# Attention of the first two batches in a new order, normalisation behind the gates, and stores on another queue

## The chip, the cores and the metric

The kernel runs on one core of a Trainium2 chip. The metric is the time of one execution on the device in microseconds (us). Below, PE is TensorE (matrix products), DVE is VectorE, ACT is ScalarE, POOL is GpSimd and SP is SyncE, which here only issues DMAs.

## The reference

Eight batches, eight heads, 576 positions (seq), head dimension 64, model width 512. Attention has no softmax, so that k and v of a head are first multiplied with each other:

```python
kv = np.einsum('bhsd,bhse->bhde', k, v)
out = np.einsum('bhsd,bhde->bhse', q, kv)
x = out / np.sqrt(np.mean(out * out, axis=-1, keepdims=True) + 1e-6) * g_norm   # (8, 576, 512)
# gated part: a causal convolution of 5 taps along seq, for each channel
gate = 1 / (1 + np.exp(-sum(conv_w[k] * xp[:, k:k + S] for k in range(5))))
x = gate * (x @ w_val) @ w_out
# second part
theta = x @ w_theta
y = w_tok_r @ (x * cos(theta)) + w_tok_i @ (x * sin(theta))
u = x + y
out = u + np.maximum(u @ w_ch, 0)
```

q, k, v arrive as float32, the weights as float64.

## The kernel before

Everything is held transposed, with channels on partitions: x of a batch is a tile of 128 partitions by 4 channel blocks by 576 positions. A weight is loaded in four chunks; each chunk comes as 64-bit words and is decoded to float32 on DVE by integer operations (`decode`, L94 to L96 and L98, with one ACT pass at L97), and then split in a high and a low part (`parts`, L68 on ACT and L69 on DVE; the names end in h and l). Every large product is made of three matmuls, high by high, high by low and low by high (`product`, L274 to L276).

The span has two parts. The first makes x, the gate and the w_out result of each batch, and stores the latter to DRAM (yd). The second loads these back and does theta, the mixing of positions and w_ch; the change does not touch it. In the first part the loop over batches i runs, for each i:

- four v products (`value`, L274 to L276 with `wv`; 24 matmuls for each of four channel blocks m). Behind each, DVE multiplies the product by the gate (L288), and ACT and DVE split it (gh, gl). The gate of a block is one ACT copy (L263), four taps on DVE (L265) and a sigmoid on ACT (L266).
- between them, attention of batch i+2: kvp (`key_value`, L182, 80 small matmuls, copied to kvs by ACT at L185) ahead of v1; o (L200, 4 groups of 8 matmuls) in two steps, the second behind the last v; ACT squares each o (L204) and copies it, scaled by g_norm (gsb), into x (L205).
- x of batch i+1 is normalised (`normalize`). For batches 0 and 1 the inverse root is spread over the partitions by matmuls (yb, L254), for the others through DRAM: a store rd (L228) and two broadcast loads yb (L233). DVE multiplies (L257 or L246), and ACT and DVE split the result in xh and xl, which the next v products read.
- four w_out products y (`first`, with `wo`). y0 and y1 first take three of their four input blocks and then the fourth. ACT copies y to yo (L304), and SP stores it (L305). After y1, `between` makes the sums of squares of batch i+2 (ss, L212) and the chain of eleven small DVE operations that makes the inverse root (L219 to L225).
- a chunk of w_theta and up to three pieces of w_tok are decoded with a low priority, the latter to be stored to DRAM (td).

Ahead of the loop stand the loads (the order is the string START: k blocks carry k and v of a pair of heads, q blocks q, v and o chunks of `wv` and `wo`, c the taps), key_value(0), three of `wv`'s four chunks, the taps, attention(0), normalize(0), then key_value(1) and attention(1). Loads of k and v use four buffers, of q two. The four PSUM tiles of this part (pool pd) are handed out in turn. A scheduler keeps the order of priorities of the code, and places an operation where its engine is free by its estimates; `issue_after` holds operations behind a named instruction. All DMAs of this part but a few are issued by SP.

## Time and profile before

| | |
|---|---|
| median of 3 runs | 753.28 us (752.94 to 756.45) |
| the profiled execution's own time | 753.31 us |
| its span | 751.5 us, 1.8 less than its time |
| PE busy | 709.7 us, 94% |
| DVE busy | 523.9 us, 70% |
| ACT busy | 335.9 us, 45% |
| start of the first v product | 48.53 us |
| start of the second part | 315.2 us |

The page gives busy times over the span. A row of the windows answer has the stretch, its length, busy time (and instructions) of PE, PE's weight loads, DVE, ACT and POOL, PE's granted clock as a share of full speed, the share of the DMA engines that was busy, and GB/s. A row of waits has who waited for whom, the total us, how often, and the longest. A timeline row has the start, the duration, the engine, the line and the operation, and in brackets how long the engine had been idle and what released it. A row of the chain of waits has start, duration and what it was. A row of groups has the line, the operation with its shape, its count, then the busy time in us and the mean ns of one. A row of DMA issues ends with the size of one and the median us from issue to landing.

### The profile page before, as it was taken

The page shows a single profiled execution, that of the slowest core. Times are in us where ns is not written, and L with a number is a line of the kernel's source. Part 1 is how long each engine was busy: PE and PEld are TensorE (multiplying, and loading weights), DVE is VectorE, ACT ScalarE, POOL GpSimd, SP SyncE. Part 2 cuts the span into 40 slices and gives each one's busy share as a digit, 9 for nine tenths or more (in the row PEclk, how much of TensorE's full clock was granted, in tenths as well). Part 3 has the DMA queues.
Part 4 walks back from the last instruction along what each step waited for, and adds up shares of the span by engine and source line. Part 5 has one row for each costly group of instructions (what it writes and reads, how often), then busy time and mean ns, then how long its engine had stood idle before and what let it go on. Part 6 is the DMA issues. An engine that isn't in the chain of part 4 may idle for free.

```text
span 751.5 us, 14674 instructions
## 1 busy us (share of the span) xinstructions
PE 709.7 (94%) x6000; PEld 669.9 (89%) x6000; DVE 523.9 (70%) x930; ACT 335.9 (45%) x560; POOL 20.7 (3%) x72
## 2 busy tenths in 40 slices
PE   1679999999989999889999999999999999999998
PEld 1568999798987999879899899999999998998998
DVE  6389969798879999588983872853853835836504
ACT  2366565637464645376541640621622514514301
POOL 4000000000000000000000000000000000000000
PEclk9779999999999999999999999999999999999999
DMA  9948794979896358534345034163051270160101
GB/s 256 285 140 243 209 229 141 229 228 237 219 238 189 108 136 246 190 102 122 111 138 157 9 119 113 32 174 90 17 164 59 69 179 35 64 175 1 64 1 64
DMA packets 77059, 104.88 MB, mean 140 GB/s; under 512 B 11712, under 2 KB 42560, under 8 KB 76992
## 3 DMA queue, kind: packets, MB, share of 16 engines
q1 hardware_dynamic: 76416, 101.85, 48.5%
q0 software_dynamic: 576, 2.10, 0.9%
q8 instruction: 47, 0.77, 0.4%
q14 instruction: 20, 0.16, 0.1%
HBM read 72.73 MB, written 31.19 MB: 138 GB/s over the span
## 4 chain that ended last, share of the span: by engine, by line
PE 60%; DVE 24%; DMA 8%; ACT 4%; issue 3%; SPq 1%; POOL 0%; DVEq 0%; ACTq 0%; POOLq 0%
PE u L513 10%; PE u L511 10%; PE u L512 10%; DVE acc L265 10%; PE c L276 5%; PE c L274 5%; PE c L275 5%; DMA yb<-rd 4%; PE th L459 3%; PE th L457 3%; PE th L458 3%; DMA kv<-in_kvm_dram 2%; DVE x L246 2%; DVE xl L69 2%; DVE acc L288 2%
## 5 line engine op out<-in xcount | busy, mean ns | idle before, releaser
L516 DVE TENSOR_TENSOR f<-u,f 128x288 f32<-128x288 f32 x64 | 26.5, 455 | 129.8 <-PE u L513 129.8
L265 DVE SCALAR_TENSOR_TENSOR acc<-x,cw,acc 128x576 f32<-128x576 f32 x128 | 100.8, 817 | 1.3 <-ACT acc L263 1.3
L68 ACT ACTIVATE uh<-f 128x288 fp32r<-128x288 f32 x64 | 26.2, 444 | 152.4 <-DVE f L516 152.3
L274 PE MATMUL y<-gh,woh 128*128 128x288 f32 x256 | 77.8, 304 | 7.8 <-DVE acc L288 5.4
L274 PE MATMUL v<-xh,wvh 128*128 128x288 f32 x256 | 77.6, 303 | 0.7 <-DVE acc L288 0.7
L276 PE MATMUL v<-xl,wvh 128*128 128x288 f32 x256 | 76.5, 299 | 0.0
L276 PE MATMUL y<-gl,woh 128*128 128x288 f32 x256 | 75.8, 298 | 0.5 <-DVE gl L69 0.5
L275 PE MATMUL y<-gh,wol 128*128 128x288 f32 x256 | 76.0, 297 | 0.0
L275 PE MATMUL v<-xh,wvl 128*128 128x288 f32 x256 | 76.0, 297 | 0.0
L274 PE MATMUL c<-uh,wch 128*128 128x288 f32 x256 | 75.4, 295 | 0.0
L276 PE MATMUL c<-ul,wch 128*128 128x288 f32 x256 | 75.4, 295 | 0.0
L275 PE MATMUL c<-uh,wcl 128*128 128x288 f32 x256 | 75.4, 294 | 0.0
L274 PEld LDWEIGHTS y<-gh,woh 128*128 128x128 f32 x256 | 48.8, 191 | 11.9 <-DVE acc L288 6.1
L274 PEld LDWEIGHTS v<-xh,wvh 128*128 128x128 f32 x256 | 48.7, 190 | 4.6 <-issue 1.7
L459 PE MATMUL th<-wth,yl 128*128 128x512 f32 x128 | 50.3, 393 | 0.0
L458 PE MATMUL th<-wtl,yh 128*128 128x512 f32 x128 | 50.1, 391 | 0.0
L457 PE MATMUL th<-wth,yh 128*128 128x512 f32 x128 | 50.0, 391 | 0.0
L276 PEld LDWEIGHTS y<-gl,woh 128*128 128x128 f32 x256 | 48.4, 190 | 1.2 <-DVE gl L69 1.2
L276 PEld LDWEIGHTS v<-xl,wvh 128*128 128x128 f32 x256 | 48.6, 190 | 0.3 <-issue 0.2
L275 PEld LDWEIGHTS y<-gh,wol 128*128 128x128 f32 x256 | 48.8, 191 | 0.0
L275 PEld LDWEIGHTS v<-xh,wvl 128*128 128x128 f32 x256 | 48.7, 190 | 0.0
L275 PEld LDWEIGHTS c<-uh,wcl 128*128 128x128 f32 x256 | 48.0, 188 | 0.3
(188 smaller groups left out, 1946.0 us busy)
## 6 DMA issues: line engine op xcount, KB each, us to landing
kv<-in_kvm_dram SPq DMA_DIRECT2D x32, 512.0 KB, 8.6
q<-in_qt_dram SPq DMA_DIRECT2D x32, 288.0 KB, 8.9
yd<-yo SPq DMA_DIRECT2D x32, 288.0 KB, 2.4
f<-yd SPq DMA_DIRECT2D x32, 288.0 KB, 3.7
out_dram<-f SPq DMA_DIRECT2D x64, 144.0 KB, 1.8
sd<-fT SPq DMA_DIRECT2D x64, 128.0 KB, 2.5
yt<-sd SPq DMA_DIRECT2D x8, 1024.0 KB, 5.6
yb<-rd SPq DMA_DIRECT2D x12, 576.0 KB, 8.0
```

What stands on the lines that cost most here:

```text
L68: one = nc.scalar.activation(h, src, AF.Copy)
L265: nc.vector.scalar_tensor_tensor(a, x[:, m, k:k + S], cw[:, m * 5 + k:m * 5 + k + 1], a, ALU.mult, ALU.add)
L274: nc.tensor.matmul(ps, wh[:, m, ks], xh[:, k, tsl], start=(k == 0), stop=False)
L275: nc.tensor.matmul(ps, wl[:, m, ks], xh[:, k, tsl], start=False, stop=False)
L276: nc.tensor.matmul(ps, wh[:, m, ks], xl[:, k, tsl], start=False, stop=(k == 3))
L457: nc.tensor.matmul(ps, yh[:, k, :], wth[0][:, k, :], start=(k == 0), stop=False)
L458: nc.tensor.matmul(ps, yh[:, k, :], wth[1][:, k, :], start=False, stop=False)
L459: nc.tensor.matmul(ps, yl[:, k, :], wth[0][:, k, :], start=False, stop=(k == 3))
L511: nc.tensor.matmul(ps[:, :HS], zh[:, ms], wkh[:, j, sl], start=(i == 0), stop=False)
L512: nc.tensor.matmul(ps[:, :HS], zh[:, ms], wkl[:, j, sl], start=False, stop=False)
L513: nc.tensor.matmul(ps[:, :HS], zl[:, ms], wkh[:, j, sl], start=False, stop=(i == 8))
L516: nc.vector.tensor_tensor(f[:, m, sl], ps[:, :HS], f[:, m, sl], ALU.add)
```

## The change

- The loads start in another order: q's first pairs come ahead of the third k block, and only chunk 0 of `wv` ahead of k and q. gsb is loaded by ACT's queue.
- key_value(0) copies each half of kvp to kvs as soon as it is done, and attention(0) goes by pairs of heads (g) in the outer loop, so that its first two o groups need only the first half. For batch 0 the scaled copy of o into x is on DVE, the squares stay on ACT.
- Of `wv` only chunk 0 is decoded ahead of attention(0). Chunks 1 to 3 come behind normalize(0), in turn with the taps of batch 0.
- key_value(1) and attention(1), which stood ahead of the first v product, are now between the v products of batch 0: key_value(1) behind the second, the two steps of o around the fourth. Loads of batch 2 follow key_value(1).
- normalize(i+1) is held behind the last split of the gated product (gs[2][-1]), and the chunks of `wo` behind the second one.
- ss and the inverse root of batch i+2 come ahead of the last chunk of y0 and y1.
- The stores of yo and of decoded w_tok are issued by ACT's queue.

The diff, cut to its core (the loop over n in attention replaces those over h and g):

```diff
-START = "v0 k0 k1 v1 k2 k3 v2 q0 q1 q2 q3 c0 v3 o0 k4 k5 k6 k7 o1 q4 q5 q6 q7 o2 o3"
-WVFIRST = 3
+START = "v0 k0 k1 q0 q1 k2 k3 q2 q3 v1 c0 v2 v3 k4 k5 k6 k7 o0 q4 q5 q6 q7 o1 o2 o3"
...
+            if b == 0 or g == 1:
+                gs = slice(2 * g if b == 0 else 0, 2 * g + 2)
+                nc.scalar.activation(kvs_of[b][:, gs, :], ps[:, 0:NP * D].rearrange("p (a e) -> p a e", e=D)[:, gs], AF.Copy)
...
+        for n in range(4):
+            g, h = divmod(n, 2) if b == 0 else (n % 2, n // 2)
...
+            if b == 0:
+                nc.vector.tensor_scalar(xo, o, gsb, None, ALU.mult)
+            else:
+                nc.scalar.activation(xo, o, AF.Copy, scale=gsb)
+            if n % 2:
+                yield x
...
-                nc.sync.dma_start(out=ydram[b][:, m, :], in_=yo)
+                nc.scalar.dma_start(out=ydram[b][:, m, :], in_=yo)
         part(0, range(3))
         part(1, range(3))
+        between()
         part(0, (3,))
         part(1, (3,))
-        between()
...
     key_value(0, kvs.pop(0))
-    for k in range(WVFIRST):
-        weight_chunk(px, wv, w_val, k, "wv", raw=raw[f"v{k}"])
+    weight_chunk(px, wv, w_val, 0, "wv", raw=raw["v0"])
+    *_, xy = attention(0, qs)
+    *_, (xs, last) = normalize(0, *xy)
     nc.vector.tensor_copy(cw, decode(px, raw["c0"], NM * 5, "cw", "c"))
-    *_, xy = attention(0, qs.pop(0))
-    *_, (xs, last) = normalize(0, *xy)
-    key_value(1, kvs.pop(1))
-    *_, xy = attention(1, qs.pop(1))
-    sg = [conv(0, m, xs[0]) for m in range(EARLY)]
-    with tc.issue_after(last.ins):
-        for n in range(WVFIRST, 4):
+    sg = []
+    for n in range(1, NM):
+        with tc.issue_after(last.ins):
             weight_chunk(px, wv, w_val, n, "wv", raw=raw[f"v{n}"])
-    kvs[2], qs[2] = load_kv(2), load_q(2)
+        if n <= EARLY:
+            sg.append(conv(0, n - 1, xs[0]))
...
+        def between(m, done):
+            if i == 0 and m == 2:
+                with tc.issue_after(done.ins):
+                    key_value(1, kvs.pop(1))
...
+        if i == 0:
+            *_, xy = second
+            kvs[2], qs[2] = load_kv(2), load_q(2)
+            key_value(2, kvs.pop(2))
+            kvs[3] = load_kv(3)
+            next(ahead)
...
-            *_, (nxs, last) = normalize(i + 1, *xy)
+            with tc.issue_after(gs[2][-1].ins):
+                *_, (nxs, last) = normalize(i + 1, *xy)
         if i == 0:
-            for k in range(4):
-                weight_chunk(px, wo, w_out, k, "wo", raw=raw[f"o{k}"])
+            with tc.issue_after(gs[2][1].ins):
+                for k in range(4):
+                    weight_chunk(px, wo, w_out, k, "wo", raw=raw[f"o{k}"])
...
-                for _ in range(RATE[0] if i < 6 else 8):
+                for _ in range(RATE[0]):
...
-                        nc.sync.dma_start(out=tokdram[:, sl], in_=decode(px, raw, sl.stop - sl.start, f"tk_{j}"))
+                        nc.scalar.dma_start(out=tokdram[:, sl], in_=decode(px, raw, sl.stop - sl.start, f"tk_{j}"))
```

Three places show what the scheduler makes of it. In the rows, names end in the batch, the block m and a running number. First, DVE in the head, from the normalisation of batch 0 on, before (acc0_0 is the gate of batch 0's block 0 in the making, L265 its taps):

```order
L257 TENSOR_TENSOR x0_282<-yb0_0_0_367,x0_282 128x2x288
L257 TENSOR_TENSOR x0_282<-yb0_0_1_377,x0_282 128x2x288
L257 TENSOR_TENSOR x0_282<-yb0_1_0_389,x0_282 128x2x288
L69 TENSOR_TENSOR xl0_366<-x0_282,xh0_365 128x4x288
L257 TENSOR_TENSOR x0_282<-yb0_1_1_399,x0_282 128x2x288
L265 SCALAR_TENSOR_TENSOR acc0_0_537<-x0_282,cw_61,acc0_0_537 128x576
L265 SCALAR_TENSOR_TENSOR acc0_1_544<-x0_282,cw_61,acc0_1_544 128x576
L69 TENSOR_TENSOR xl0_366<-x0_282,xh0_365 128x4x288
L265 SCALAR_TENSOR_TENSOR acc0_0_537<-x0_282,cw_61,acc0_0_537 128x576
L265 SCALAR_TENSOR_TENSOR acc0_1_544<-x0_282,cw_61,acc0_1_544 128x576
L265 SCALAR_TENSOR_TENSOR acc0_0_537<-x0_282,cw_61,acc0_0_537 128x576
```

and now (wv_1 is chunk 1 of `wv`; L271 are the taps, L93 to L97 the decode, L68 the splits):

```order
L263 TENSOR_TENSOR x0_260<-yb0_0_1_355,x0_260 128x2x288
L263 TENSOR_TENSOR x0_260<-yb0_1_0_367,x0_260 128x2x288
L68 TENSOR_TENSOR xl0_344<-x0_260,xh0_343 128x4x288
L263 TENSOR_TENSOR x0_260<-yb0_1_1_377,x0_260 128x2x288
L93 TENSOR_SCALAR dst_wv_1_396<-raw_wv_1_170 128x512
L271 SCALAR_TENSOR_TENSOR acc0_0_404<-x0_260,cw_61,acc0_0_404 128x576
L94 SCALAR_TENSOR_TENSOR dst_wv_1_396<-raw_wv_1_170,dst_wv_1_396 128x512
L68 TENSOR_TENSOR xl0_344<-x0_260,xh0_343 128x4x288
L95 SCALAR_TENSOR_TENSOR dst_wv_1_396<-raw_wv_1_170,dst_wv_1_396 128x512
L271 SCALAR_TENSOR_TENSOR acc0_0_404<-x0_260,cw_61,acc0_0_404 128x576
L97 SCALAR_TENSOR_TENSOR dst_wv_1_396<-raw_wv_1_170,dst_wv_1_396 128x512
L271 SCALAR_TENSOR_TENSOR acc0_0_404<-x0_260,cw_61,acc0_0_404 128x576
```

Between the taps of the first gate now stands the decode of `wv`'s chunk 1, which before had been made ahead of the normalisation.

Second, DVE at the end of batch 1's v products, before (L288 are the gates, L246 the normalisation of x of batch 2, dst_wt a chunk of w_theta):

```order
L288 TENSOR_TENSOR acc1_2_1095<-v1_2_1196,acc1_2_1095 128x576
L69 TENSOR_TENSOR gl1_1066<-acc1_2_1095,gh1_1065 128x576
L246 TENSOR_TENSOR x2_740<-x2_740,yb2_992 128x4x288 x2
L94 TENSOR_SCALAR dst_wt_0_1481<-raw_wt_0_1479 128x512
L288 TENSOR_TENSOR acc1_3_1189<-v1_3_1242,acc1_3_1189 128x576
L95 SCALAR_TENSOR_TENSOR dst_wt_0_1481<-raw_wt_0_1479,dst_wt_0_1481 128x512
L69 TENSOR_TENSOR xl2_1293<-x2_740,xh2_1292 128x4x288
L69 TENSOR_TENSOR gl1_1066<-acc1_3_1189,gh1_1065 128x576
L69 TENSOR_TENSOR xl2_1293<-x2_740,xh2_1292 128x4x288
```

and now (L296 are the gates, L252 the normalisation):

```order
L296 TENSOR_TENSOR acc1_2_1096<-v1_2_1197,acc1_2_1096 128x576
L68 TENSOR_TENSOR gl1_1067<-acc1_2_1096,gh1_1066 128x576
L296 TENSOR_TENSOR acc1_3_1190<-v1_3_1243,acc1_3_1190 128x576
L68 TENSOR_TENSOR gl1_1067<-acc1_3_1190,gh1_1066 128x576
L252 TENSOR_TENSOR x2_769<-x2_769,yb2_975 128x4x288 x2
L93 TENSOR_SCALAR dst_wt_0_1482<-raw_wt_0_1480 128x512
L68 TENSOR_TENSOR xl2_1294<-x2_769,xh2_1293 128x4x288 x2
L271 SCALAR_TENSOR_TENSOR acc2_0_1466<-x2_769,cw_61,acc2_0_1466 128x576
```

The normalisation, which reads yb2, has moved from ahead of the last gate to behind the last split.

Third, ACT in batch 1's w_out products, before (L304 copies y to yo, L266 are the sigmoids of batch 2's gates):

```order
L304 ACTIVATE yo1_0_1344<-y1_0_1300 128x576
L304 ACTIVATE yo1_1_1353<-y1_1_1319 128x576
L266 ACTIVATE acc2_0_1465<-acc2_0_1465 128x576
L266 ACTIVATE acc2_1_1472<-acc2_1_1472 128x576
L304 ACTIVATE yo1_2_1434<-y1_2_1409 128x576
L266 ACTIVATE acc2_2_1546<-acc2_2_1546 128x576
L304 ACTIVATE yo1_3_1462<-y1_3_1437 128x576
L266 ACTIVATE acc2_3_1640<-acc2_3_1640 128x576
```

and now (L313 are the stores, L272 the sigmoids):

```order
L312 ACTIVATE yo1_0_1398<-y1_0_1301 128x576
L313 DMA yd1_71<-yo1_0_1398 128x576
L312 ACTIVATE yo1_1_1407<-y1_1_1320 128x576
L313 DMA yd1_71<-yo1_1_1407 128x576
L272 ACTIVATE acc2_0_1466<-acc2_0_1466 128x576
L312 ACTIVATE yo1_2_1435<-y1_2_1410 128x576
L313 DMA yd1_71<-yo1_2_1435 128x576
L272 ACTIVATE acc2_1_1473<-acc2_1_1473 128x576
L312 ACTIVATE yo1_3_1463<-y1_3_1438 128x576
L313 DMA yd1_71<-yo1_3_1463 128x576
L272 ACTIVATE acc2_2_1547<-acc2_2_1547 128x576
```

Each store stands right behind its copy, ahead of the next copy and of the sigmoids.

More of the change, by code (lines that the diff above doesn't have):

```diff
@@ L173, in key_value @@
         ps = one_bank(f"kvp{b}")
+        kvs_of[b] = pa.tile([P, NP, D], F32, tag="kvs", bufs=2, name=f"kvs{b}")
         for g in range(2):
@@ L183, in key_value, with attention @@
                                          start=(c == 0), stop=(c == 4), tile_position=(0, j * D))
-        kvs_of[b] = pa.tile([P, NP, D], F32, tag="kvs", bufs=2, name=f"kvs{b}")
-        nc.scalar.activation(kvs_of[b], ps[:, 0:NP * D].rearrange("p (a e) -> p a e", e=D), AF.Copy)
-    def attention(b, q):
-        kv = kvs_of.pop(b)
+            if b == 0 or g == 1:
+                gs = slice(2 * g if b == 0 else 0, 2 * g + 2)
+                nc.scalar.activation(kvs_of[b][:, gs, :], ps[:, 0:NP * D].rearrange("p (a e) -> p a e", e=D)[:, gs], AF.Copy)
+    def attention(b, qs):
+        kv, q = kvs_of.pop(b), qs.pop(b)
         x = pa.tile([P, NM, PAD + S], F32, tag="x", bufs=2, name=f"x{b}")
@@ L275, in product @@
             nc.tensor.matmul(ps, wl[:, m, ks], xh[:, k, tsl], start=False, stop=False)
-            nc.tensor.matmul(ps, wh[:, m, ks], xl[:, k, tsl], start=False, stop=(k == 3))
+            done = nc.tensor.matmul(ps, wh[:, m, ks], xl[:, k, tsl], start=False, stop=(k == 3))
+        return done
     def value(b, x, xh, xl, sg, between):
@@ L280, in value @@
         gl = pa.tile([P, NM, S], F32R, tag="gl", bufs=1, name=f"gl{b}")
+        lasts, done = [], None
         for m in range(NM):
-            between(m)
+            between(m, done)
             g = sg[m]
@@ L285, in value @@
             for h in range(2):
-                product(ps[:, h], wv, m, xh, xl, h * HS)
+                done = product(ps[:, h], wv, m, xh, xl, h * HS)
             halves = lambda t: t.rearrange("p (h s) -> p h s", h=2)
             nc.vector.tensor_tensor(halves(g), ps, halves(g), ALU.mult)
-            parts(gh[:, m, :], gl[:, m, :], g)
+            lasts.append(parts(gh[:, m, :], gl[:, m, :], g)[0])
             if m + EARLY < NM:
                 sg.append(conv(b, m + EARLY, x))
-        return gh, gl
+        return gh, gl, lasts
     def first(b, gh, gl, between):
@@ L362, in attention_moe_holo_kernel @@
     raw = {}
+    nc.scalar.dma_start(out=gsb[0:D], in_=gn)
+    nc.scalar.dma_start(out=gsb[D:P], in_=gn)
     for what in START.split():
@@ L401, in attention_moe_holo_kernel @@
         if two:
-            ahead = attention(i + 2, qs.pop(i + 2))
-        def between(m):
-            if two and m == 1:
+            ahead = attention(i + 2, qs)
+        def between(m, done):
+            if i == 0 and m == 2:
+                with tc.issue_after(done.ins):
+                    key_value(1, kvs.pop(1))
+            if two and i and m == 1:
                 key_value(i + 2, kvs.pop(i + 2))
@@ L410, in between @@
             if two and m == 3:
-                next(ahead)
+                next(ahead if i else second)
+        second = attention(1, qs) if i == 0 else None
         gs = value(i, *xs, sg, between)
+        if i == 0:
[4 more added lines that the diff above has]
+            next(ahead)
         if two:
@@ L418, in attention_moe_holo_kernel @@
         if i + 1 < B:
-            *_, (nxs, last) = normalize(i + 1, *xy)
+            with tc.issue_after(gs[2][-1].ins):
+                *_, (nxs, last) = normalize(i + 1, *xy)
         if i == 0:
-            for k in range(4):
-                weight_chunk(px, wo, w_out, k, "wo", raw=raw[f"o{k}"])
+            with tc.issue_after(gs[2][1].ins):
+                for k in range(4):
+                    weight_chunk(px, wo, w_out, k, "wo", raw=raw[f"o{k}"])
         got = []
-        first(i, *gs, lambda: got.append(next(ahead) if two else None))
+        first(i, *gs[:2], lambda: got.append(next(ahead) if two else None))
         xy = got[-1]
@@ L434, in attention_moe_holo_kernel @@
                         weight_chunk(px, w, src, k, name, scale)
-                for _ in range(RATE[1] if i < 6 else 11):
+                for _ in range(RATE[1]):
                     if toks:
```

24 lines of the change are left out of this document (9 added, 15 removed).

## Prediction

> **What bounds the kernel now.** I read the page first (which engine is full), then one windows answer cut at the starts of the eight v products, then PE's waits, and last the timeline at the places where PE waits. PE is TensorE, DVE is VectorE, ACT is ScalarE.
>
> ```profile
> span 751.5 us, 14674 instructions
> PE 709.7 (94%) x6000; PEld 669.9 (89%) x6000; DVE 523.9 (70%) x930; ACT 335.9 (45%) x560; POOL 20.7 (3%) x72
> ```
>
> PE is idle for 751.5 − 709.7 = 41.8 us in all: with the same products a new order wins no more, except where PE's clock is low. The windows answer has one row for the head (up to the first v product), one for each batch 0 to 7, and one for the second part:
>
> ```profile
> 0.00:48.50 48.50, 22.51 (x384) 18.68 (x384) 28.52 (x51) 20.37 (x33) 10.90 (x42) 0.88 0.94 258
> 48.50:89.50 41.00, 40.89 (x466) 36.57 (x465) 38.07 (x74) 24.75 (x40) 1.51 (x5) 0.94 0.74 199
> 89.50:121.60 32.10, 32.10 (x370) 30.05 (x369) 25.96 (x45) 18.18 (x28) 1.18 (x5) 1.00 0.73 187
> 121.60:155.80 34.20, 32.68 (x370) 30.09 (x369) 29.58 (x51) 19.48 (x30) 1.19 (x5) 1.00 0.85 219
> 155.80:189.00 33.20, 32.42 (x370) 29.97 (x370) 29.98 (x51) 19.34 (x31) 1.80 (x5) 1.00 0.84 223
> 189.00:224.10 35.10, 32.39 (x370) 30.04 (x369) 27.70 (x48) 18.02 (x28) 1.45 (x5) 1.00 0.89 223
> 224.10:258.90 34.80, 32.79 (x370) 30.05 (x370) 34.45 (x62) 21.41 (x34) 0.39 (x1) 1.00 0.52 159
> 258.90:286.10 27.20, 25.96 (x194) 25.49 (x193) 25.66 (x44) 14.18 (x23) 0.00 (x0) 1.00 0.51 146
> 286.10:315.20 29.10, 27.18 (x194) 26.95 (x193) 22.48 (x33) 10.75 (x17) 1.22 (x2) 0.94 0.68 211
> 315.20:751.50 436.30, 430.75 (x2930) 412.00 (x2928) 261.50 (x484) 169.42 (x301) 1.06 (x2) 1.00 0.31 91
> ```
>
> Of a row I use the length and the busy times of PE, DVE and ACT. Over half of the span is the second part, which the change leaves alone. The head has 26 us of idle PE. Batch 1 takes 32.10 us with PE busy throughout, so 32.10 is what a batch costs without a gap; batches 2 to 5 take 2.1, 1.1, 3.0 and 2.7 more, 8.9 together. Batches 6 and 7 (no attention left to compute) have 1.24 and 1.92 us of idle PE.
>
> PE's waits name the owners:
>
> ```profile
> PE kvp L182 <- DMA kv<-in_kvm_dram: 16.0, 4, 6.6
> PE y L274 <- DVE acc L288: 5.4, 3, 2.5
> PE ss L212 <- ACT sq L204: 4.7, 3, 3.3
> ```
>
> **Part 1, the head.** The chain up to the first v product, from the chain of waits and the timeline:
>
> ```profile
> 2.54 6.00 DMA kv<-in_kvm_dram
> 8.55 10.79 DMA kv<-in_kvm_dram
> 19.38 2.41 PE kvp L182 x38
> 22.25 2.62 PE L200 MATMUL o<-q,kvs 64*64 64x288 f32 x32 [0.47 <-ACT kvs L185]
> 23.43 0.65 ACT L204 ACTIVATE sq<-o 128x576 f32<-128x576 f32 x1 [1.23 <-PE o L200]
> 28.02 0.78 ACT L205 ACTIVATE x<-o,gsb 128x576 f32<-128x576 f32 x1
> 28.22 0.69 PE L212 MATMUL ss<-sq,ind 128*32 128x72 f32 x28 [0.85 <-ACT sq L204]
> 31.97 4.79 PE L254 MATMUL yb<-y,sel 32*128 32x72 f32 x64 [3.06 <-DVE y L225]
> 37.00 1.36 DVE L69 TENSOR_TENSOR xl<-x,xh 128x1152 fp32r<-128x1152 f32 x1 [0.30 <-ACT xh L68]
> ```
>
> ACT makes four squares (0.65) and four scaled copies (0.78) in a row, and the second half of ss waits for the last square. Now the copies go to DVE, and the first pairs' squares are done before the fourth k block lands. That landing ended at 19.34; I put it at 18.3, an estimate, since a weight chunk less shares the queue with it. From there: half of kvp 2.4, a copy of kvs 0.4, the first o 0.6 (a quarter of 2.62), two squares 1.3, the last ss 0.7, which ends at 23.7; with q's second pairs a little later, 24.2. The rsqrt chain (3.06) then ends at 27.25, where it ended at 31.97: 4.7 earlier (3.7 if the landing stays). Normalisation takes as long as it did (31.97 to the end of the first xl at 38.36), so v0_0 can start at about 33.7. It started at 48.53:
>
> ```profile
> 36.69 4.10 PE L182 MATMUL kvp<-kv 128*64 128x64 f32 x80
> 41.30 2.22 PE L200 MATMUL o<-q,kvs 64*64 64x288 f32 x32 [0.51 <-ACT kvs L185]
> 47.43 1.17 PE L212 MATMUL ss<-sq,ind 128*32 128x72 f32 x28 [3.31 <-ACT sq L204]
> 48.53 0.61 PE L274 MATMUL v<-xh,wvh 128*128 128x288 f32 x1
> ```
>
> PE's clock under that kvp is the third number from the right, 0.50:
>
> ```profile
> 36.00:38.00 2.00, 2.00 (x32) 1.87 (x32) 1.70 (x2) 2.00 (x3) 0.00 (x0) 0.50 0.91 202
> ```
>
> So the first v product moves 14.8 us ahead, and with it the wait of 3.31 goes. But kvp1, o1 and ss1 now come behind it: 2.4 (kvp at full clock; 3.3 of its 4.10 here are at half clock), 2.2 and about 0.7, some 5.3 us. If PE alone set the pace, 14.8 − 5.3 = 9.5 would be won. It doesn't, for DVE is full over the same stretch:
>
> ```profile
> 34.00:95.30 61.30, 57.10 (x754) 51.01 (x752) 57.63 (x102) 36.31 (x56) 3.10 (x12) 0.89 0.71 195
> ```
>
> The price of a decode, from the groups by shape (mean ns of one behind the busy time):
>
> ```profile
> L95 DVE SCALAR_TENSOR_TENSOR dst_tk<-raw_tk,dst_tk 128x512 int32<-128x512 int32 x10 | 6.9, 692 | 0.1
> L94 DVE TENSOR_SCALAR dst_tk<-raw_tk 128x512 int32<-128x512 int32 x10 | 4.2, 425 | 0.0
> ```
>
> DVE idles for 61.30 − 57.63 = 3.67 us from its first read of yb to the last tap of batch 1. That work (normalisation, taps, gates, decodes) now starts 4.7 earlier, but two more decodes stand in it. Only wv's chunk 0 is decoded early now; the early ones cost nothing, since DVE had nothing else then. A decode is five passes, one of 0.425 and four of 0.692; neighbours overlap by about 0.08 (each starts before the last one's end), so 0.35 + 4 × 0.61 = 2.8. So 5.6 us come in, and the end of the stretch moves by −4.7 + 5.6 = +0.9 if it keeps its idle time, and by 0.9 − 3.67 = −2.8 if it loses all of it. PE's earlier start lets DVE lose most, as the gates find their products done: I take −1.6. Instead, PE will wait for wvl and for gates between the products of batch 0.
>
> The 0.94 in batch 0's row is a low clock:
>
> ```profile
> 48.00:50.00 2.00, 2.00 (x24) 1.56 (x13) 2.00 (x4) 2.00 (x5) 0.00 (x0) 0.50 0.28 99
> ```
>
> It follows PE's wait of 3.31 and lasts into v0; the first v product after a shorter wait may keep its clock, which DVE's bound hides either way. The Trainium skill (TensorE: Matmul & The Clock Gate, section "Part 1: The HAM clock gate (the "warmup" mystery)") says that the clock is halved after an idle window of about 3.4 us and released after as long of sustained work. This row agrees, after a wait of 3.31; by the rule a cold start of v0 would cost an estimated 1.7 us.
>
> **Part 2, batches 1 to 5.** Batch 4 shows the excess:
>
> ```profile
> 209.07 2.63 DVE L246 TENSOR_TENSOR x<-x,yb 128x1152 f32<-128x1152 f32 x2 [3.40 <-DMA yb<-rd]
> 211.62 0.75 DVE L288 TENSOR_TENSOR acc<-v,acc 128x576 f32<-128x576 f32 x1
> 212.43 0.40 PE L274 MATMUL y<-gh,woh 128*128 128x288 f32 x1 [2.51 <-DVE acc L288]
> ```
>
> The normalisation of the next batch stands ahead of the last gate on DVE: DVE waits 3.40 for the broadcast yb, multiplies for 2.63, and only then gates; y waits 2.51 for that gate. Now the gates come first, and y needs nothing of the normalisation. Next v needs xl: gate, gh and gl 2.2 (three passes of 0.75), then 2.63 and about 3.8 for xh and two xl of 1.36, 8.6 us behind the last v product. Beside it run y's four tiles of 3.24 each (25.96 in batch 6 is eight such tiles), 13.0, and ss: over 4 us are spare, which also cover yb's wait of 3.40. And rd is sent before y0's last chunk, with no kv load between rd and yb on SP's queue. If that cover went, the next v would wait for what is left of yb. DVE's load in batches 1 to 4 is 25.96 to 29.98 of 32.10, so its queue drains in each batch; I leave 0.3 us of loose joints in each of 2, 3 and 4: 2.1 + 1.1 + 3.0 − 0.9 = 5.3 won. Batch 5 has 34.45 of DVE, and by the order keeps about as much: 34.45 − 32.10 = 2.35 stays of its 2.7, 0.35 won. Together 5.65. Bounds: all 8.9, or nothing if each wait moves to v.
>
> **Part 3, batches 6 and 7.**
>
> ```profile
> 274.95 0.75 DVE L288 TENSOR_TENSOR acc<-v,acc 128x576 f32<-128x576 f32 x1
> 302.51 0.40 PE L274 MATMUL y<-gh,woh 128*128 128x288 f32 x1 [1.92 <-DVE acc L288]
> ```
>
> In batch 6 the last gate (274.95) stands in the order behind passes that decode w_tok; in batch 7 the taps are late and PE waits 1.92, after which PE's clock halves (0.94 in that row). The order now has 10 fewer decode passes between the last gates of batches 5 and 6, 10 × 0.61 = 6.1 us less ahead of those taps, more than the wait. Batch 6 wins 1.0 of its 1.24, batch 7 its distance to batch 6's busy time: 29.10 − 25.96 = 3.1, of which I take 2.9. Bounds: 0 and 4.4.
>
> **Part 4, the stores.** 32 stores of yo and the decoded tokens go to ACT's queue. SP loses the issues:
>
> ```profile
> yd<-yo SPq DMA_DIRECT2D x32, 288.0 KB, 2.4
> q<-in_qt_dram SPq DMA_DIRECT2D x32, 288.0 KB, 8.9
> ```
>
> SP isn't on PE's path in those stages, and what waited behind a store there was the next loads, which land in time. ACT must wait for its own copy to end and issue; its load is 18 to 21 us of 32.10, so I count nothing. No row shows a store from ACT. Below, the bound is the 0.3 a batch that I left in part 2, if yb leaves earlier still; above, ACT waits out the landing of each, 4 × 2.4 = 9.6 a batch, which its 11 to 14 free us still cover. I take nothing, as neither end reaches PE. The Trainium skill (DMA: Bandwidth & Descriptors, section "Issuing engines are not separate DMA queues") says that transfers started by different engines share the same 16 DMA engines, and only time on the issuing sequencer is saved. By that the transfers themselves gain nothing; no row of before can show it, and the sum counts nothing for them.
>
> **The sum.** 1.6 + 5.65 + 1.0 + 2.9 = 11.15 us off the profiled execution, whose own time is 753.31 (1.8 beside its span, 0.03 above the median of the runs): 742.2. Bounds of the terms together: a loss of 0.9, or a gain of 2.8 + 8.9 + 4.4 = 16.1: 754.2 and 737.2.
>
> **The rivals.** *PE sets the head alone:* DVE's idle time disappears, and the decodes fit in gaps between taps, so that the head gives 9.5 instead of 1.6: 734.3. Against it is DVE's row (57.63 of 61.30). Chance 0.07. *The work is only moved:* DVE's total is unchanged, so the stalls come back at v, which then waits for xl in place of y for the gate; only the head's 1.6 and 1.2 of batches 6 and 7 remain: 750.5. For it speaks DVE's 34.45 in batch 5, against it the 2 to 6 us a batch that DVE has spare in batches 1 to 4. Chance 0.14. *k and v of batch 2 come late:* their loads now go out only when kvp1, behind v0_1, has freed the buffers, and kvp2 wants them two v tiles, o1 and ss1 later, some 10 us, where a k block took 6.0 to 10.8 to land; with the 6.6 us wait of kvp's row as a worst case, 4.5 lost: 746.7. Chance 0.08.
>
> *Slower: ACT is held at its stores.* In this trace a transfer starts only when the eighth before it has landed: the chain has one issued at 2.54 landing at 8.54, and the k block that comes eight transfers later issued at 8.55. A store that follows a q or kv load by eight would hold ACT until that lands, and copies of y (which free PSUM tiles), squares and sigmoids queue behind it. It decides where the stores of a batch wait more than about 9.6 us together (y2, y3 and the next v0, 3 × 3.2, pass before v1 wants a tile whose copy is held). With one landing of 8.9 and half of a second, 13.4 − 9.6 = 3.8 lost in each of six batches, 22.8: 765. Against it: the stores come late in y, when the loads of their batch have had 10 us to land. Chance 0.05.
>
> **How the numbers follow.** The forecast has 0.66, with its own range of 737 to 747. 0.5% is 3.8 us, about what a measurement of this kernel can tell from no change: faster is below 749.5, slower above 757.1. Faster: 0.65 of the forecast, the first rival's 0.07, the third's 0.07, 0.02 of the second: 0.81. Same: 0.12 of the second, 0.01 and 0.01 of the forecast and the third: 0.14. Slower: 0.05. The range leaves out ACT's rival (0.05), most of the first (0.06) and the upper half of the second: 735 to 751.
>
> **What would show it.** In the profile after: v0_0 near 34, but v1_0 only 1 to 3 us before 89.56; DVE still full from about 29 to 94; no y waiting for a gate in batches 1 to 4 and no wait of DVE for yb ahead of a gate; batches 2 to 4 near 32.4 each; no low clock in batch 7; a second part of 436.3. I am wrong if v1_0 starts before 84 (PE's head), if v waits for xl by over 1 us a batch, or if ACT's idle time names its own DMA issues.

## The result and the profile after

The changed kernel takes 758.44 us (median of 8 runs, 757.11 to 759.91) where the kernel before takes 754.98 (8 runs, 752.16 to 756.51): a ratio of 1.0053, with a 95% interval of 1.0032 to 1.0074. It is slower by half a per cent, where I had forecast 742.2. The profiled execution took 758.88, 5.6 us more than that of before (753.31).

The page of the changed kernel starts so:

```profile
span 757.1 us, 14657 instructions
PE 716.5 (95%) x6000; PEld 673.2 (89%) x6000; DVE 527.1 (70%) x934; ACT 334.8 (44%) x557; POOL 19.2 (3%) x72
```

PE is busy 6.8 us longer with the same 6000 matmuls, so part of the loss is a lower clock. The windows answer, cut at the starts of the v products as before (head, batches 0 to 7, second part; the head now ends at 33.8, so batch 0 holds what had been ahead of it):

```profile
0.00:33.80 33.80, 16.85 (x240) 12.63 (x240) 13.84 (x30) 7.24 (x13) 9.49 (x38) 0.81 0.96 268
33.80:91.30 57.50, 50.86 (x608) 44.07 (x609) 54.90 (x100) 35.65 (x56) 2.35 (x9) 0.88 0.72 207
91.30:123.40 32.10, 32.10 (x370) 30.05 (x369) 24.38 (x40) 17.71 (x27) 1.23 (x5) 1.00 0.68 187
123.40:155.50 32.10, 32.10 (x370) 30.05 (x369) 31.01 (x53) 19.04 (x30) 1.23 (x5) 1.00 0.83 236
155.50:193.80 38.30, 34.74 (x370) 31.45 (x369) 30.54 (x53) 20.66 (x32) 1.24 (x5) 0.91 0.75 221
193.80:234.10 40.30, 35.02 (x370) 31.86 (x369) 31.95 (x56) 20.54 (x32) 1.23 (x5) 0.92 0.68 204
234.10:268.20 34.10, 32.41 (x370) 29.94 (x369) 31.89 (x56) 20.68 (x33) 0.12 (x1) 1.00 0.40 119
268.20:295.20 27.00, 26.05 (x194) 25.58 (x193) 24.77 (x40) 12.98 (x20) 0.00 (x0) 1.00 0.66 198
295.20:322.80 27.60, 25.82 (x195) 25.56 (x194) 22.87 (x34) 11.66 (x18) 1.22 (x2) 1.00 0.70 206
322.80:757.10 434.30, 430.52 (x2930) 411.99 (x2928) 260.96 (x484) 168.64 (x300) 1.05 (x2) 1.00 0.30 89
```

Against the rows of before: head and batch 0 together 91.3 instead of 89.5 (+1.8), batch 1 as it was, batch 2 −2.1, batch 3 +5.1, batch 4 +5.2, batch 5 −0.7, batch 6 −0.2, batch 7 −1.5, the second part −2.0. These make +5.6, all of the difference. The loss is in batches 3 and 4: PE idles there for 3.6 and 5.3 us, and is busy 2.6 and 2.9 us longer than in batch 1, at a mean clock of 0.91 and 0.92. The head has a low clock too (0.88 in the row of batch 0): 4.3 of PE's 6.8 us lie ahead of batch 1 (67.7 us busy there, 63.4 before).

PE's and DVE's waits name who is late. In the kernel before, DVE waited for yb:

```profile
DVE x L246 <- DMA yb<-rd: 6.2, 3, 3.4
```

and now:

```profile
PE o L202 <- DVE acc L296: 7.2, 2, 4.3
PE y L280 <- DVE acc L296: 1.8, 1, 1.8
...
DVE dst_tk L93 <- DMA td<-dst_tk: 6.9, 2, 5.0
DVE dst_wt L93 <- DMA td<-dst_tk: 5.6, 1, 5.6
```

The wait of y for a gate has shrunk as forecast (5.4 before), and in its place o waits for one. And DVE now waits 12.5 us for stores of decoded w_tok (td) to land. The timeline of batch 3 shows the chain (ACTq is ScalarE's DMA queue; the number ahead of the engine is the duration):

```profile
164.79 0.33 ACTq L458 DMA_DIRECT2D td<-dst_tk  x1
172.87 0.43 DVE L93 TENSOR_SCALAR dst_tk<-raw_tk 128x512 int32<-128x512 int32 x1 [5.05 <-DMA td<-dst_tk]
174.48 0.75 DVE L296 TENSOR_TENSOR acc<-v,acc 128x576 f32<-128x576 f32 x1
175.29 1.24 PE L202 MATMUL o<-q,kvs 64*64 64x288 f32 x8 [2.85 <-DVE acc L296]
```

and the windows answer PE's clock behind it:

```profile
176.00:178.00 2.00, 1.29 (x16) 0.30 (x8) 1.23 (x2) 2.00 (x5) 0.00 (x0) 0.50 0.06 9
```

A store goes out at 164.79, in the middle of the loads of k and v, and lands 8.1 us later. The decode of the piece after next (a w_theta chunk takes the other buffer in between) wants the same one of two buffers (dst), so its first pass waits 5.05 us for that landing; the gate of v behind it on DVE comes at 174.48, and o waits 2.85 for the PSUM tile that the gate frees. PE's clock then falls to 0.50. The Trainium skill (TensorE: Matmul & The Clock Gate, section "Part 1: The HAM clock gate (the "warmup" mystery)") says that the clock is halved after a window of about 3.4 us without work; here a wait of 2.85 was enough, so the trace differs. Nor does the length of a single wait decide it: the 1.8 that y waits in batch 7 left the clock alone, while in the kernel before a wait of 1.92 in batch 7 halved it and one of 2.51 in batch 4 did not (0.94 and 1.00 in their rows).

### The profile page after: what moved, and what is told of

Same layout as the page of the kernel before. It is cut to its first block, busy times and chain, and to the rows that moved or that the text cites. A ratio compares the mean times of both kernels' runs of the same rounds, so it can differ in the third digit from the quotient of the medians.

```text
span 757.1 us, 14657 instructions
## 1 busy us (share of the span) xinstructions
PE 716.5 (95%) x6000; PEld 673.2 (89%) x6000; DVE 527.1 (70%) x934; ACT 334.8 (44%) x557; POOL 19.2 (3%) x72
## 4 chain that ended last, share of the span: by engine, by line
PE 60%; DVE 22%; DMA 9%; ACT 5%; issue 2%; SPq 0%; ACTq 0%; DVEq 0%
PE u L531 10%; PE u L529 10%; PE u L530 10%; DVE acc L271 9%; PE c L280 4%; PE c L281 4%; PE c L282 4%; PE th L477 3%; PE th L475 3%; PE th L476 3%; DMA td<-dst_tk 3%; DMA kv<-in_kvm_dram 2%; DVE xl L68 2%; DVE acc L296 2%; DVE gl L68 1%
## 5 line engine op out<-in xcount | busy, mean ns | idle before, releaser
L271 DVE SCALAR_TENSOR_TENSOR acc<-x,cw,acc 128x576 f32<-128x576 f32 x128 | 102.7, 814 | 1.0 <-ACT acc L269 0.9
```

Source lines behind the costliest of these rows:

```text
L271: nc.vector.scalar_tensor_tensor(a, x[:, m, k:k + S], cw[:, m * 5 + k:m * 5 + k + 1], a, ALU.mult, ALU.add)
```

## The experiments

My theory after the profile: two buffers and the landing of the store make the wait. The rival: ScalarE's queue itself costs, as its stores hold ScalarE up. All ratios are against the kernel before, run on the same chip at the same time; its median was 752.75 to 755.41 in the six sessions.

### The stores

**e1: three buffers for decoded weights.**

```diff
-        dst = pool.tile(..., bufs=(1 if tag else 2) if pool is px else 1, ...)
+        dst = pool.tile(..., bufs=(1 if tag else 3) if pool is px else 1, ...)
```

> The changed kernel with three buffers for decoded weights (dst) instead of two, nothing else. Theory: in batches 3 and 4 DVE waits 5.05 and some 5.6 us for a store of decoded w_tok to land, because the next decode takes one of only two buffers, and the last gates stand behind that wait. With three buffers the store that was waited for is one that landed long ago: the waits of DVE for td go from 12.5 us to under 2, batches 3 and 4 (38.3 and 40.3 us) come to 32 to 34, and the time falls by 9 to 12 us, to 747 to 750. Rival: ScalarE's queue holds ScalarE up at its stores, so that squares, copies and the PSUM tiles come late: a buffer more changes nothing, batches 3 and 4 stay above 37, time 756 to 760.

Measured: 746.23 us, ratio 0.9898 (0.9866 to 0.9929). The windows rows of batches 2 to 5 and of the second part:

```profile
122.10:154.20 32.10, 32.10 (x370) 30.05 (x369) 30.92 (x53) 19.11 (x30) 1.24 (x5) 1.00 0.84 241
154.20:186.30 32.10, 32.10 (x370) 30.05 (x369) 31.12 (x54) 20.10 (x31) 1.24 (x5) 1.00 0.86 253
186.30:218.50 32.20, 32.15 (x370) 30.03 (x369) 29.07 (x51) 20.30 (x31) 1.24 (x5) 1.00 0.85 245
218.50:253.30 34.80, 32.73 (x370) 30.05 (x369) 33.27 (x59) 21.26 (x33) 0.12 (x1) 1.00 0.43 132
308.30:742.90 434.60, 430.87 (x2930) 412.00 (x2928) 261.09 (x484) 168.59 (x300) 1.06 (x2) 1.00 0.30 89
```

The one wait of DVE for td that is left:

```profile
DVE dst_wt L93 <- DMA td<-dst_tk: 1.5, 1, 1.5
```

With every store still on ScalarE's queue, batches 3 and 4 become 6.2 and 8.1 us shorter, and PE has no gap in batches 2 and 3. The store of batch 3 goes out at 163.48 and still lands 7.8 us later, but the next decode has begun at 163.69 in another buffer. ScalarE itself does wait for the landing of w_out results (yo has two buffers as well), and longer than in the changed kernel (6.0):

```profile
ACT yo L312 <- DMA yd<-yo: 14.1, 6, 3.9
```

PE pays nothing for that wait in batches 2 to 4. So the rival falls; the buffer is the cause.

**e2: the stores of w_tok back on SP** (`nc.sync` for `nc.scalar` at L458).

> The changed kernel with only the stores of decoded w_tok put back on SP's queue. Theory (DVE waits for the landing of such a store, whatever queue it is on): on SP the store of batch 3 stands behind the loads of k, v and q and goes out later than the 164.8 us of the changed kernel, so DVE's wait in batch 3 grows from 5 to about 10 us and that batch goes above 41; in batch 4 the order has no decode of w_theta behind such a store, so it comes to 32 to 35; time 752 to 757. Rival (ScalarE's queue is what costs): both batches come back to 32 to 34, time 747 to 750.

Measured: 747.23 us, 0.9926 (0.9894 to 0.9958): the rival's number, and not the one that I had worked out from the theory. Batches 3 and 4, from the windows answer:

```profile
156.00:188.10 32.10, 32.10 (x370) 30.05 (x369) 29.55 (x50) 20.14 (x31) 1.24 (x5) 1.00 0.88 253
188.10:221.10 33.00, 32.45 (x370) 29.93 (x369) 30.37 (x53) 18.95 (x29) 1.24 (x5) 1.00 0.83 231
```

The decode that had waited, from the timeline:

```profile
170.36 0.42 DVE L93 TENSOR_SCALAR dst_tk<-raw_tk 128x512 int32<-128x512 int32 x1
```

The landing times of the stores of L458:

```profile
DMA to landing us min/median/max: 2.0/6.7/8.1
```

The stores land no sooner than on ScalarE's queue (median 6.7, after the change 5.4). But nobody waits: the decode now starts behind the last pass of a w_theta chunk, whose buffer has no store to wait for. In the order of the changed kernel that pass stood behind it. The store of the piece before goes out only at 176.28, so this decode can't stand in its buffer: with SP the scheduler picks another one, where my expectation had assumed the same. The Trainium skill (DMA: Bandwidth & Descriptors, section "Issuing engines are not separate DMA queues") says that DMAs of all issuing engines run on the same 16 DMA engines, and that only the time of issuing is saved. The landing times don't speak against it: on ScalarE's queue alone the medians run from 5.4 us after the change to 8.9 in e4, and SP's 6.7 lies between.

**e3: the stores of the w_out results back on SP** (L313), those of w_tok on ScalarE.

> The changed kernel with only the stores of the w_out results put back on SP's queue. Theory: batches 3 and 4 keep the waits of DVE for td, 37 us or more each; the second part, 434.3 us after the change and 436.3 before, comes back to 436, as its loads wait behind the stores on SP; time 758 to 762. Rival (ScalarE's queue, with its 32 stores, is what costs): batches 3 and 4 come to 33 to 35, time 748 to 752.

Measured: 761.98 us, 1.0101 (1.0062 to 1.0141). Batch 3 and the second part:

```profile
156.80:196.20 39.40, 35.02 (x370) 31.71 (x369) 30.80 (x54) 19.88 (x32) 1.24 (x5) 0.91 0.76 216
324.70:761.30 436.60, 430.76 (x2930) 412.00 (x2929) 261.54 (x484) 169.17 (x301) 1.06 (x2) 1.00 0.31 91
```

As the theory has it: the 32 stores on ScalarE's queue cost the first part nothing, and win some 2 us in the second.

**e4: the kernel before with both kinds of stores on ScalarE's queue**, and **e12: the same with three buffers.**

> The kernel before with both kinds of stores put on ScalarE's queue, nothing else. Theory: the stores alone cost nothing, as in the order of before no decode ahead of a gate takes the buffer of a store that is just going out; the second part wins up to 2 us; time 750 to 755. Rival (ScalarE's queue costs): batches 3 and 4 grow by 3 us or more each, time 759 or more.

> The kernel before with both kinds of stores on ScalarE's queue and three dst buffers. With two it took 769.3 us, and DVE waited 13.5 us for stores of decoded w_tok. Theory (the buffer makes the wait): the waits for td are under 2 us, the batches of over 40 us come back under 36, time 749 to 755. Rival (ScalarE's queue costs in the old order whatever the buffers): time over 760.

Measured: e4 769.26 us, 1.0207 (1.0158 to 1.0255), the rival's side; e12 751.39, 0.9973 (0.9952 to 0.9995), the theory's. Of e4, DVE's wait:

```profile
DVE dst_tk L94 <- DMA td<-dst_tk: 13.5, 2, 7.0
```

and batch 2, from the windows answer:

```profile
120.90:163.50 42.60, 35.76 (x370) 32.46 (x370) 34.74 (x61) 21.04 (x32) 1.19 (x5) 0.88 0.73 215
```

I had thought the old order safe. It isn't, once the stores are on ScalarE's queue: the third piece's decode then stands at 140.91, behind a wait of 6.6 us, and not at 160.96 as in the kernel before. It looks as if the scheduler reckoned with an early landing; no run shows what it reckons with. Two buffers and such stores cost 15 us there, and a third buffer takes 18 away.

### The hold of the normalisation

**e8: the changed kernel with three buffers, without the hold** (`issue_after(gs[2][-1].ins)` taken away around normalize).

> The changed kernel with three dst buffers and without the hold of normalize(i+1). Theory (the hold is what wins in batches 2 to 4): they go from 32.1 back to 33 to 35, together 4 to 6 us, time 750 to 753. Rival (the inverse root ahead of y's last chunk and the emptier SP queue bring yb early enough anyway): they stay at 32.1 to 32.5, time 745 to 747.5.

Measured: 753.29 us, 1.0003 (0.9977 to 1.0029). DVE waits for yb again:

```profile
DVE x L252 <- DMA yb<-rd: 10.3, 6, 5.0
```

Batch 2, from the windows answer:

```profile
124.30:157.60 33.30, 32.32 (x370) 30.03 (x369) 30.34 (x51) 18.95 (x29) 1.24 (x5) 1.00 0.90 235
```

Batches 2 to 4 take 33.3, 33.8 and 34.3 where e1 has 32.1, 32.1 and 32.2: the hold wins 5.0 us there, and 7 to 8 in all against e1.

**e7: the kernel before with the hold alone; e15: with the w_out stores on ScalarE's queue too; e17: with the w_tok stores there instead, and three buffers.**

```diff
-            *_, (nxs, last) = normalize(i + 1, *xy)
+            with tc.issue_after(gs[2].ins):
+                *_, (nxs, last) = normalize(i + 1, *xy)
```

(`gs[2]` is here the last split, gl on DVE; e15 has `nc.scalar` at L305, e17 at L440 and bufs 3.)

> The kernel before with one thing of the change: normalize(i+1) is held behind the last split of the gated product. Theory: DVE no longer waits for yb ahead of the last gate; batches 2 to 4 (34.2, 33.2 and 35.1 us before) come to 32.1 to 32.6 each, batch 5 stays over 33.5; time 746 to 750 against some 754. Rival (the work is only moved): v then waits for xl, batches 2 to 4 stay over 33, time 752 to 755.

> The kernel before with two things of the change: normalize(i+1) is held behind the last split, and the stores of the w_out results go out on ScalarE's queue (those of decoded w_tok stay on SP's). With the hold alone the first part ended 8 us earlier, but PE waited 12.86 us in the second part for w_tok, whose loads stood on SP's queue. Theory (the loads behind the stores on SP's queue give the hold's gain back): the wait of PE for wkh falls under 3 us, the second part comes back from 448.3 to 434 to 437, time 744 to 748. Rival (the second part can't start earlier because of its own loads, whatever queue the stores are on): the wait stays over 8 us, time 753 or more.

> The kernel before with three things: normalize(i+1) held behind the last split, the stores of decoded w_tok on ScalarE's queue (those of the w_out results stay on SP's), and three dst buffers. Theory (with the hold, the last store of w_tok goes out at 291 to 295 us on SP's queue, and the second part's first loads stand behind it): the first loads of the w_out results go out before 280 us, PE's wait for wkh falls under 4 us, the second part takes 434 to 438, time 745 to 749. Rival (the second part's loads are late for another reason): the second part stays over 444 us, time 753 or more.

Measured: e7 757.31 us, 1.0072 (1.0045 to 1.0099), outside both expectations, though its batches 2 and 3 came to 32.1 and batch 4 to 33.4; e15 754.12, 1.0006 (0.9982 to 1.0031), the rival's; e17 747.24, 0.9893 (0.9857 to 0.9929), the theory's. In e7 the second part starts at 307.1, 8.1 earlier than before, but takes 448.3, from the windows answer:

```profile
307.10:755.40 448.30, 432.07 (x2930) 413.35 (x2929) 263.86 (x488) 170.50 (x303) 1.47 (x3) 0.98 0.32 96
```

From the timeline, the last pass of w_tok's last decode, its store, the first loads of the second part, and PE's wait:

```profile
290.62 0.21 DVE L98 SCALAR_TENSOR_TENSOR dst_tk<-raw_tk,dst_tk 128x64 f32<-128x64 f32 x1
290.86 0.32 SPq L441 DMA_DIRECT2D td<-dst_tk  x1
291.23 1.85 SPq L330 DMA_DIRECT2D f<-yd  x4
...
333.96 0.61 PE L512 MATMUL u<-wkh,zht 128*128 128x288 f32 x1 [12.86 <-ACT wkh L68]
```

The last pass of that decode now comes late on DVE; its store goes out at 290.86 (in the kernel before at 275.06), and the first loads of the second part stand right behind it on SP's queue. In e17 that store is on ScalarE's queue, and the timeline has the pass and these loads at

```profile
268.06 0.23 DVE L98 SCALAR_TENSOR_TENSOR dst_tk<-raw_tk,dst_tk 128x64 f32<-128x64 f32 x1
268.43 0.80 SPq L330 DMA_DIRECT2D f<-yd  x2
```

PE's wait for wkh, from the waits, is down to

```profile
PE u L512 <- ACT wkh L68: 2.4, 2, 1.3
```

The hold keeps its gain. What stood in the way is the late store of w_tok, not those of w_out (e15). That ScalarE's queue is the cure isn't shown: the third buffer came with it, and the pass itself ends 22.5 us sooner in e17, so that its store could have gone out in time on SP's queue too. In e2, with the hold and these stores on SP's queue, the loads stand at

```profile
277.70 2.26 SPq L338 DMA_DIRECT2D f<-yd  x4
```

and PE waits 0.5 us for wkh. e17 shows one thing more: it has the head of the kernel before and batches 2 to 4 of 32.1 each, and its ratio of 0.9893 can't be told from e1's 0.9898. The new order of the head wins nothing by itself: the first v product of batch 1 comes at 88.9 to 91.5 us in the six traces with the old one (before, e4, e7, e12, e15, e17), and at 90.0 to 93.5 in the six with the new one as it is (after, e1, e2, e3, e8, e16).

**e16: e1 with the w_out stores back on SP.**

> The changed kernel with three dst buffers and the stores of the w_out results put back on SP's queue. Theory (the stores on SP's queue cost more, the earlier the second part starts): the second part, 434.6 us with three dst buffers, takes 437 to 447; time 748 to 758. Rival: it takes under 437, as where only these stores were put back (436.6), time 746 to 748.

Measured: 748.61 us, 0.9923 (0.9894 to 0.9951); the second part took 436.3. That is the rival's side, though the time lies just above its range, and inside the theory's: these stores are worth some 2 us, as in e3, and no more.

### The head

**e5: e1 with the last pass of the decode left out for w_val and w_out; e6: e1 with chunks 1 and 2 of w_val decoded ahead of attention(0)** (START "v0 k0 k1 v1 q0 q1 k2 k3 v2 q2 q3 c0 v3 ..." from e1's).

(`tiny` is false for these two weights alone.)

```diff
-        nc.scalar.activation(hi.bitcast(F32), hi.bitcast(F32), AF.Square)
-        nc.vector.scalar_tensor_tensor(dst, hi.bitcast(F32), TINY, dst, ALU.is_ge, ALU.mult)
+        if tiny:
+            nc.scalar.activation(hi.bitcast(F32), hi.bitcast(F32), AF.Square)
+            nc.vector.scalar_tensor_tensor(dst, hi.bitcast(F32), TINY, dst, ALU.is_ge, ALU.mult)
```

> The changed kernel with three dst buffers, and the last integer-decode pass on DVE (with its square on ScalarE) left out for w_val and w_out: weights too small for float32 are not set to zero. Seven decodes, three of w_val and four of w_out, lie between the first product of batch 0 and that of batch 1, so 7 x 0.61 = 4.3 us of DVE's work go there and nothing else. Theory (DVE's work sets the head): the first v product of batch 1, at 90.0 us with three buffers, starts 3.0 to 4.5 us earlier, and the time falls by as much from the 746.2 of that kernel, to 742 to 743.5. Rival (PE's half clock, the late landing of k and the chain of batch 1 set it): that product stays within 1 us of 90.0, time 745.5 to 747.

> The changed kernel with three dst buffers, and chunks 1 and 2 of w_val decoded ahead of attention(0) again, as before the change; their loads stand ahead of the third k block and of q's second pairs. Theory (DVE's work sets the head): 5.6 us leave DVE's stretch, and the chain of batch 0 starts 2 to 3 us later as a chunk of 0.5 MB more is loaded ahead of it; the first v product of batch 1 comes at 86.5 to 88.5 instead of 90.0, time 743 to 745. Rival: only the later loads count, that product comes at 91 to 93, time 747 to 749.

Measured: e5 745.03 us, 0.9898 (0.9873 to 0.9923), the rival's side; e6 744.43, 0.9892 (0.9858 to 0.9926). e6's time lies in the theory's range by luck, for its ratio can't be told from e1's and its product keeps to neither range. The first v product of batch 1 came at 90.83 in e5 and 90.64 in e6, not before the 90.02 of e1. So DVE's work alone, which I had held to be the bound, doesn't set it. In e5 another wait has come up:

```profile
PE o L203 <- DMA q<-in_qt_dram: 2.6, 1, 2.6
```

The last q block of batch 2 landed at 68.23, and o of batch 2, on which yb of batch 1 waits in PE's order, came only then. In e1 that yb, at 70.20, had waited 2.72 us for DVE's rsqrt chain instead.

**e9: e1 with q of batch 2 in yb's buffer, loaded early; e10: e9 without the pass; e11: e9 with w_val early.**

```diff
+            if b == 2:
+                if p == 0:
+                    whole = px.tile([P, NM, S], F32, tag="yb", bufs=1, name="q2")
+                    q += [whole[:, 0:2, :], whole[:, 2:4, :]]
-            if j == 0:
+            elif j == 0:
...
+    qs[2] = load_q(2)
     todo = [(wth, w_th, k, "wt", 1.0 / TWO_PI) for k in range(4)]
```

> The changed kernel with three dst buffers, and q of batch 2 loaded into the buffer that yb uses from batch 2 on, so that it needn't wait for attention(1) to free q's two buffers; its load stands ahead of that of batch 2's k and v. Theory after the two runs before (two bounds of the same height: DVE's work, and q of batch 2, whose last block landed at 66 to 68 us): q early alone moves nothing, the first v product of batch 1 stays at 89 to 90.5 and the time at 745 to 747. Rival (q's landing alone sets the head): that product comes 2 to 3 us earlier, time 742.5 to 744.

> The kernel with q of batch 2 loaded early, and the last integer-decode pass left out for w_val and w_out as well (weights too small for float32 are not set to zero). Theory (two bounds of the same height): with both gone the first v product of batch 1 comes 3 to 4.3 us earlier than 90.0, at 85.7 to 87, time 741.5 to 743.5. Rival (a third thing, such as k and v of batch 2 landing at 60 or the half clock of PE, sets the head): it stays at 89 or later, time 744.5 or more.

> The kernel with q of batch 2 loaded early, and chunks 1 and 2 of w_val decoded ahead of attention(0) as before the change. Theory (two bounds of the same height): 5.6 us of DVE's work leave the stretch, the chain of batch 0 starts 5 us later as in the run with w_val early alone (first product at 39.5); the first v product of batch 1 comes at 86.5 to 89, time 741.5 to 744. Rival: that product stays over 90, time 744 to 746.

Measured: e9 747.93 us, 0.9928 (0.9906 to 0.9950); e10 745.00, 0.9893 (0.9860 to 0.9927); e11 744.67, 0.9885 (0.9850 to 0.9920). The product came at 93.02, 91.03 and 92.15: all miss the theory's numbers. e9 lies outside both expectations; e10 and e11 are the rivals'. The early q pushes the k and v of batch 2 back, whose last block lands at 63.9 to 68.1 in the three, and kvp waits in e10 (16.6 us in all, 12.3 in e1).

**e13: q, k and v of batch 2 all loaded early; e14: the same without the pass.**

```diff
-            if i == 0 and m == 2:
-                with tc.issue_after(done.ins):
-                    key_value(1, kvs.pop(1))
+            if i == 0 and m == 0:
+                key_value(1, kvs.pop(1))
+                kvs[2] = load_kv(2)
+                for k in range(4):
+                    raw[f"o{k}"] = fetch(px, w_out[:, k, :], DM, f"wo_{k}")
```

(START ends in "q4 q5 q6 q7 q8 q9 q10 q11", the last four being q of batch 2.)

> The changed kernel with three dst buffers, q of batch 2 loaded into yb's buffer right behind q of batch 1, key_value(1) ahead of the first v product (so that the loads of batch 2's k and v go out some 6 us earlier), and the loads of w_out behind these. Theory (the head of the changed kernel is set by two things of the same height, DVE's work and the landing of batch 2's q, k and v): with the loads early DVE's work still sets it, the first v product of batch 1 stays at 88.5 to 91, time 744.5 to 747. Rival (the landings alone set it): 85 to 87.5, time 741 to 744.

> The same with the last integer-decode pass left out for w_val and w_out (weights too small for float32 are not set to zero). Theory: both bounds are gone, the first v product of batch 1 comes at 85 to 87.5 and the time is 740.5 to 743.5. Rival (a third bound, in PE's half clock or ScalarE): it stays at 89 or later, time 744 or more.

Measured: e13 748.95 us, 0.9933 (0.9908 to 0.9959); e14 742.73, 0.9853 (0.9822 to 0.9884). The first v product of batch 1, first in e13:

```profile
94.33 0.29 PE L285 MATMUL v<-xh,wvh 128*128 128x288 f32 x1
```

and in e14:

```profile
86.92 0.29 PE L285 MATMUL v<-xh,wvh 128*128 128x288 f32 x1
```

k and v of batch 2 land by 50.8 and 51.1. With the loads out of the way, the seven passes less move the product by 7.4 us (1.2 of it because e14's head began sooner), more than the 4.3 that they are worth, and with the loads late (e1 to e5) they moved it by nothing. Nearly all of it stands ahead of yb of batch 1, at 74.09 in e13 and 67.07 in e14. So two things of about the same height set when that yb comes, DVE's work and batch 2's loads: one wait in e1, the other in e5, and both gone in e14. e14 fits its number. e13's product comes 3 us behind its range and its time is 2 us above: products of batch 0 wait there 3.8 us for the decoded w_val, which my expectation had left out. As e13 also moves kvp of batch 1 and the loads of `wo`, it isn't e1 with early loads alone, and that the two are of the same height rests on e1, e5 and e14.

## Why the prediction was wrong

- **What bounds the kernel:** right in the batches. The time lies where PE waits, and DVE's order decides it. In the head PE's clock had a share that I had left out (part 1).
- **Part 4, the stores: the step that failed.** I wrote "I take nothing, as neither end reaches PE", after bounding what a store could cost ScalarE. The cost was not on ScalarE's row. DVE waited for the landing of the w_tok stores (12.5 us), because the decode behind one needs its buffer, and the gate stands behind the decode. I took the slower case to be ScalarE held at its stores. ScalarE does wait for w_out results to land (8.0 us after the change, 16.1 in e1), but e1 leaves all stores there and gains 1.5%. The two traces have these stores, on SP's queue before and on ScalarE's after, with size and median landing:

```profile
td<-dst_tk SPq DMA_DIRECT2D x10, 256.0 KB, 2.8
td<-dst_tk ACTq DMA_DIRECT2D x10, 256.0 KB, 5.4
```

  In the trace of before nobody waited for them; I never asked who reuses their buffer.
- **Part 2, batches 1 to 5:** right in mechanism and size, once that wait is gone. e1 has 32.1, 32.1 and 32.2 for batches 2 to 4 (I had 32.4), and 34.8 for batch 5 (34.45). The hold does it (e8). In the changed kernel itself only batch 2 shows the gain; in 3 and 4 the wait for td outweighs it.
- **Part 1, the head:** the first v product came at 33.82 where I had 33.7, by luck. The rsqrt chain ended at 28.8, 3.1 earlier than before and not 4.7, as the fourth k block landed at 19.29, no sooner than before. And the product waited for xh alone, where I had put it behind the first xl, which ended at 35.2. The first v product of batch 1 came at 91.34 where 88.0 would have been my 1.6 of gain. DVE lost none of its idle time (3.6 us from its first read of yb to the last tap of batch 1, 3.67 before). My third rival, k and v of batch 2 late, did not hold: kvp of that batch waits for no load here. Its q was late, with two waits of 0.3 ahead of o, and behind o yb of batch 1 waited 2.15 for ScalarE's copy of it:

```profile
28.84 4.57 PE L260 MATMUL yb<-y,sel 32*128 32x72 f32 x62 [3.08 <-DVE y L231]
33.82 0.61 PE L280 MATMUL v<-xh,wvh 128*128 128x288 f32 x1 [0.19 <-ACT xh L67]
66.97 2.41 PE L202 MATMUL o<-q,kvs 64*64 64x288 f32 x24 [0.32 <-DMA q<-in_qt_dram]
71.53 4.40 PE L260 MATMUL yb<-y,sel 32*128 32x72 f32 x64 [2.15 <-ACT x L210]
91.34 0.29 PE L280 MATMUL v<-xh,wvh 128*128 128x288 f32 x1
```

  From that yb to the product PE does the same 224 matmuls in both kernels, and has no gap in the changed one. The windows rows, before and after (the first also counts four matmuls of o and the product itself):

```profile
71.69:89.56 17.87, 17.76 (x229) 17.27 (x225) 17.87 (x32) 12.54 (x19) 0.00 (x0) 1.00 0.90 242
71.53:91.34 19.81, 19.81 (x224) 19.41 (x225) 18.02 (x34) 12.09 (x18) 0.00 (x0) 0.83 0.90 247
```

  The 1.9 us more are as much as head and batch 0 lost (1.8), and DVE, full in the first row, is idle for 1.8 of the second. So here PE's low clock is what makes the head end later; I had counted no low clock there, and had trusted DVE's bound to hide one at the first v product. How far DVE would have kept up with a full clock no run shows.

- **Part 3, batches 6 and 7:** mis-sized. They won 0.2 and 1.5, not 1.0 and 2.9; the clock stays at 1.00 in batch 7 as forecast, but y still waits 1.8 for a gate.
- **The second part:** I held it unchanged at 436.3; it took 434.3. The w_out stores off SP's queue are worth these 2 us (e3, e16).
- **The sum:** with the td wait taken out, e1's profiled execution took 744.65 us, 2.5 above the forecast of 742.2. Against my lengths the first v product of batch 1 is 2.1 later, batches 2 to 4 are 0.8 shorter together, batches 5, 6 and 7 are 0.35, 0.8 and 1.8 longer, and the second part is 1.7 shorter: 2.55.

Four kernels that compute all of the reference have the lowest ratios to the kernel before: e11, e6, e17 and e1, with 0.9885, 0.9892, 0.9893 and 0.9898. Their intervals overlap.

## What to carry to other kernels

Where a store is moved to another queue, ask who reuses the stored buffer, and what stands behind that user on its engine: the landing time becomes a wait of an engine in order, and one buffer more can be worth more than the queue. A change of queue in one line also changes what the scheduler does with the work behind it (another buffer in e2, earlier decodes in e4), so look at the order of the waiting engine around each reuse. And when removing the bound of a stage changes nothing, look for a second one of the same height before dropping the first: here only both together (e14) moved the head forward.

## What I had not expected of the hardware

A store of 256 KB landed in a median of 2.8 us in the kernel before, where those of batches 2 to 4 went out over 7 us behind the last load of q, and in 5.4 us (at most 8.6) among the loads of k and v, on ScalarE's queue; on SP's queue, right behind the loads of q, it took 6.7 (e2). PE's clock fell to 0.50 after a wait of 2.85 us in batch 3, which cost some 2.6 us of busy time beside the idle 3.6, and a wait of 2.15 in the head brought a mean clock of 0.83 over the next 19.8 us.
